# Another written-out order for the first 18 pairs of an attention and MLP kernel, and one weight difference in two halves

## The chip, the cores and the metric

The kernel runs on one core of one Trainium2 chip. The metric is the device time of one execution in microseconds (us). All durations below come from one execution that was recorded by the profiler, or are the times of unrecorded runs where the text says so.

## The reference

Cosine attention over 8 batches of 12 heads, 448 positions and a head dimension of 64, followed by a two-layer MLP with a hard-swish between the layers. Everything comes in and goes out in float32.

```python
q_n = q / (norm(q, axis=-1) + 1e-06)            # q, k, v: (8, 12, 448, 64)
k_n = k / (norm(k, axis=-1) + 1e-06)
attn = softmax(q_n @ k_n.T / tau)                # tau = 0.1
x = (attn @ v), heads side by side               # (3584, 768)
h = x @ w_in                                     # w_in: (768, 2048)
g = h * clip(h + 3, 0, 6) / 6
out = g @ w_out                                  # w_out: (2048, 768)
```

## The kernel before, in words

**Pairs and items.** Two heads of one batch form a pair; there are 48 pairs, six to a batch. Queries and keys are loaded two pairs at a time. Each such load is an item: of the first fourteen items the even one of a twosome is q and the odd one k, so items 2d and 2d+1 serve pairs 2d and 2d+1. An item goes through these operations, named as in the plan below:

- LQ loads it (L197, SyncE's queue, 448 KB), LV loads the values of two pairs (L209, four transfers).
- SQ squares it (L224 on ACT, L226 on DVE or POOL), RE sums the squares over the head dimension (L238, DVE), NO makes the reciprocal norms of two items with four short activations (L254 to L257, ACT), NM multiplies by them into bf16 (L269, DVE or POOL).
- TR transposes it on TensorE (L314). Later items are transposed by a DMA instead (XD).
- CQ and CK, with CS for the rest of the keys, copy the transposed tiles out of PSUM (L334, L336, L364, L374).
- VC casts the values of one pair (L286 on DVE, L288 on POOL).

A pair then runs through SC.i.g, the score matmuls of its four groups of keys (L414, L417), EX.i.g, the exponentials (L435, ACT), VA.i.g, the product with the values (L457), and FI, which divides by the row sums (L477, L478, DVE). BK and CX bring the result of a pair, transposed, into the MLP's input xT (L495, L497, L336); XB and XP do it by DMA.

**The MLP.** A unit U is one step of it: six matmuls into one PSUM bank for one of sixteen tiles of the hidden layer (L568), or, for the last six of the 36 units within the plan, sixteen matmuls of the second layer (L615). UA is its first evacuation on ACT (L577), UV the one on DVE (L583, or L628), which frees the bank. A unit of the first batch needs xT of pairs 0 to 5 complete and its part of w_in loaded; W issues one of eight weight transfers from POOL's queue (L911).

**Banks.** Up to pair 5 the scores use two double banks in turn. OPEN closes these and opens a ring of six single banks, which the scores (two banks a group), the transposes and the units take in turn. TensorE waits for the next bank in the ring until whoever read it last is done.

**Strassen's products.** From batch 1 on the second layer is computed by seven products of half-size blocks instead of eight. They need sums and differences of blocks of w_out, made once on DVE: WS (L690). The sums 1, 6 and 7 have tiles of their own; the differences y3 and y4, for the products M3 and M4, overwrite blocks of w_out, and so come after the last unit that still reads those blocks. GL copies the last columns of a batch's hidden layer to the next (L559).

**What sets the order.** For pairs 0 to 17 the order is written out by hand as a list of strings, `PLAN`. Tokens are executed in the order written, each recording its instructions on its engine; an engine then works its instructions off in that order, waiting where data or buffers are missing. A token's last letter names the engine where there is a choice: p is POOL, v DVE, a ACT. `DP.n` issues n matmuls of zeros into the PV bank (L923), 248 columns each, and `D.n` n of 512 columns into Y (L918): dummies, with no use of their result. From pair 18 (`FIRST`) on a loop sets the order; the table `side` lists the extra DVE operations of each round, and in round 18 that is y4.

Of the kernel before, what the change touches and what calls it, by code (L numbers as in the profile page):

```python
# [18 lines left out]
ORDER = "111111111111111111111111111111222222"  # L19

PLAN = [
    "LQ.1 DP.5 SQ.1.a.11.3 SQ.1.p.4.3 DP.1 SQ.1.a.0.4 LQ.0 SQ.0.p.8.6 DP.2 DP.4 LQ.3 LQ.2 SQ.1.v.7.4 RE.1.1",
    "SQ.0.a.0.6 RE.1.0 NO.0.1 LQ.5 LQ.4 SQ.0.v.6.2 DP.6 NM.1.p.0 D.10 RE.0.1 DP.3 NM.1.p.1 RE.0.0 DP.8",
    "NO.0.0 SQ.3.a.0.7 LV.0 DP.2 SQ.2.a.0.7 NM.0.p.0 RE.3 RE.2 NM.0.p.1 TR.1.Y DP.2 TR.0.Z CK.0.v DP.4 SQ.4.p.0.7 CQ.0.v",
    "SQ.5.a.0.7 LQ.6 NO.1 LV.1 LQ.7 SC.0.0.0 SC.0.1.1 DP.5 DP.3 CQ.1.v EX.0.0 RE.5 RE.4 NM.3.p SC.0.2.0 CK.1.v",
    "DP.3 EX.0.1 DP.3 EX.0.2 NM.2.v DP.3 SC.0.3.1 TR.3.Y LQ.8 NO.2 EX.0.3 DP.3 SC.1.0.0 TR.2.Z EX.1.0 VC.0.v",
    "SC.1.1.1 DP.2 EX.1.1 VA.0.0 CK.2.v VC.1.v VC.3.v NM.4.p NM.5.p VA.0.1 LQ.9 SC.1.2.0 SQ.6.a.0.7 LQ.11 DP.5",
    "DP.2 SC.1.3.1 EX.1.2 CQ.2.v LQ.10 LV.2 VA.0.2 VA.0.3 DP.3 SC.2.0.0 DP.2 EX.1.3 CK.3.v SC.2.1.1 EX.2.0 TR.4.Y",
    "SC.2.2.0 SQ.7.p.0.7 EX.2.1 RE.6 FI.0 RE.7 LV.3 VA.1.0 SQ.8.p.0.7 SC.2.3.1 CQ.3.v VC.2.v CQ.5.v VA.1.1 EX.2.2",
    "SC.3.0.0 EX.2.3 VA.1.2 NO.3 RE.8 SC.3.1.1 CQ.4.v EX.3.0 DP.2 DP.4 EX.3.1 VA.1.3 TR.5.Z SC.3.2.0 W SQ.9.p.0.7",  # L30
    "EX.3.2 FI.1 CK.4.v BK.0.Y VA.2.0 SC.3.3.1 RE.9 LV.4 EX.3.3 NO.4 VA.2.1 VA.2.2 VA.2.3 SC.4.0.0 EX.4.0 NM.6.p",
    "DP.2 SC.4.1.1 SQ.10.p.0.7 W SQ.11.p.0.7 EX.4.1 CX.0.v TR.6.Y CK.5.v FI.2 CQ.7.v VA.3.0 BK.2.Z RE.10 SC.4.2.0",
    "EX.4.2 NM.7.p CQ.6.v VA.3.1 SC.4.3.1 DP.2 EX.4.3 CX.2.v SC.5.0.0 RE.11 VA.3.2 EX.5.0 SC.5.1.1 VA.3.3 VC.4.p",
    "SC.5.2.0 FI.3 VC.5.p EX.5.1 BK.1.Y TR.7.Z SC.5.3.1 CX.1.v CK.6.v CK.7.v VA.4.0 EX.5.2 DP.2 CS.7.v EX.5.3",
    "BK.3.Y VA.4.1 LQ.12 CS.6.v OPEN DP.2 CX.3.v NO.5 SC.6.0 VA.4.2 VA.4.3 SC.6.1 SC.6.2 EX.6.0 NM.8.p FI.4 EX.6.1",
    "EX.6.2 SC.6.3 TR.8 BK.4 VA.5.0 CX.4.v VA.5.1 CQ.8.v SC.7.0 VA.5.2 EX.6.3 NM.9.p CQ.9.v VC.6.p VA.5.3 SC.7.1",
    "FI.5 EX.7.0 SC.7.2 TR.9 SC.7.3 NM.10.p CK.8.v VA.6.0 EX.7.1 EX.7.2 VC.8.p CS.8.v W BK.5 SQ.12.p.0.7 LQ.13",
    "VA.6.1 VA.6.2 SC.8.0 EX.7.3 CS.9.v VA.6.3 CK.9.v DP.1 EX.8.0 CX.5.v SC.8.1 SC.8.2 VC.7.p FI.6 LQ.15 EX.8.1 U",
    "UA SQ.13.a.0.7 LV.5 U TR.10 EX.8.2 UA U RE.13 U SC.8.3 UV UA CQ.10.v VA.7.0 W RE.12 UV CQ.11.a UV UA NO.6 U",
    "EX.8.3 VA.7.1 VA.7.2 UV VC.9.p VA.7.3 NM.11.p SC.9.0 FI.7 NM.12.p UA SC.9.1 UV EX.9.0 U VA.8.0 SC.9.2 EX.9.1",  # L40
    "VC.10.p UA SC.9.3 TR.11 UV NM.13.p CS.11.v XP.6 VA.8.1 LQ.14 EX.9.2 SQ.15.a.0.7 VA.8.2 U EX.9.3 CK.11.v",
    "CK.10.v VA.8.3 SC.10.0 TR.12 U CS.10.v FI.8 UA UV VA.9.0 SC.10.1 LQ.17 EX.10.0 SQ.14.p.0.7 CQ.12.v CQ.13.v",
    "SC.10.2 UA VA.9.1 LQ.19 VA.9.2 EX.10.1 LQ.16 VA.9.3 LV.6 W UV SC.10.3 EX.10.2 U SC.11.0 FI.9 EX.10.3 SC.11.1",
    "U UA EX.11.0 LV.7 EX.11.1 UV UA SC.11.2 RE.15 BK.8 LQ.18 CX.8.v U VA.10.0 U VA.10.1 UA EX.11.2 UV UV RE.14",
    "SC.11.3 UA BK.9 VA.10.2 VA.10.3 FI.10 EX.11.3 TR.13 NO.7 CK.13.v CS.13.v CX.9.a U UV CK.12.a VC.11.p W",
    "VA.11.0 U SC.12.0 CS.12.v VA.11.1 VA.11.2 UA BK.10 VA.11.3 UV UA NM.15.p UV EX.12.0 CX.10.v SC.12.1 EX.12.1",
    "SC.12.2 FI.11 U EX.12.2 BK.11 SC.12.3 UA NM.14.p SQ.16.p.0.6 U UA CX.11.v UV U SC.13.0 SQ.17.p.0.7 XD.14 UV",
    "RE.17 EX.12.3 VC.12.p EX.13.0 SQ.16.a.6.1 U UA RE.16 VC.15.p U VA.12.0 UV XD.15 UA U UA UA UV SC.13.1",
    "SQ.19.p.0.7 VC.13.p SC.13.2 UV EX.13.1 LQ.21 U VA.12.1 VA.12.2 UA UV RE.19 VA.12.3 EX.13.2 UV NO.8 W U",
    "SC.13.3 NM.16.p CK.15.v CK.14.v U UA UA SQ.18.a.0.7 EX.13.3 U SC.14.0 FI.12 UA VA.13.0 VC.14.p CS.14.v UV",  # L50
    "VA.13.1 UV EX.14.0 UV U SC.14.1 SC.14.2 VA.13.2 VA.13.3 UA EX.14.1 UV U W SC.14.3 FI.13 U VA.14.0 NM.17.p UA",
    "EX.14.2 UA VA.14.1 EX.14.3 XD.17 U UV VA.14.2 RE.18 SC.15.0 SC.15.1 UA UV EX.15.0 U XD.16 EX.15.1 UA UV",
    "VA.14.3 SC.15.2 U UA SC.15.3 EX.15.2 FI.14 NO.9 LV.8 VA.15.0 LV.9 UV CK.16.v UV EX.15.3 U SQ.21.p.0.7 VA.15.1",
    "RE.21 CS.16.v LQ.20 SC.16.0 LQ.22 SC.16.1 UA VC.16.p SC.16.2 VC.17.p VA.15.2 EX.16.0 VA.15.3 XP.12 NM.18.v",
    "CK.17.v XD.18 U EX.16.1 SQ.20.a.0.7 NM.19.p FI.15 WS.6 U UV XD.19 SC.16.3 RE.20 GL.0 WS.1 WS.7.0 EX.16.2 U VA.16.0 UA VA.16.1 LV.11",
    "EX.16.3 SC.17.0 UV VC.19.p SC.17.1 SC.17.2 SQ.22.v.0.7 VA.16.2 LQ.23 EX.17.0 VA.16.3 EX.17.1 LV.10 U SC.17.3",
    "XP.14 NO.10 FI.16 NM.20.p CK.18.v U CK.19.v WS.7.1 WS.y3 XB.16 EX.17.2 UV UA VA.17.0 VC.18.p EX.17.3 CS.18.v",
]


# [1038 lines left out]
```

## Time and profile before

| | us |
|---|---|
| median of 3 runs | 406.69 |
| lowest and highest | 406.35, 407.81 |
| the profiled execution | 406.46 |
| its span, first to last instruction | 404.6 |
| start of the first transpose on TensorE (TR.1) | 9.32 |
| start of the first exponential (EX.0.0) | 13.13 |
| start of the first unit (U) | 43.11 |

The granted clock of TensorE is 1.000 over the span. The span is 1.86 us shorter than the execution that it belongs to.

How to read the rows that follow: a row of the timeline gives the start in us from the span's first instruction, the length of the merged group, engine, line, operation, tiles as output<-inputs, shape, how many (x18), and in brackets how long the engine had been idle before and what ended the wait. A row of the busy time by stage gives the stretch, its length, and the busy us (and number of instructions) of PE, PEld (weight loads), DVE, ACT and POOL, then TensorE's granted clock, the share of the DMA engines and GB/s. A matmul's recorded length includes the time until its result has drained, so consecutive matmuls overlap; what one costs TensorE is the distance between two starts.

### The profile page before, as it was taken

What the parts mean: (1) busy time and instruction counts of PE and PEld (TensorE: products, weight loads), DVE (VectorE), ACT (ScalarE), POOL (GpSimd) and SP (SyncE); (2) the same over time, 40 slices, a digit from 0 to 9 for tenths busy, and PEclk for the clock granted to TensorE, in tenths of its full rate; (3) what the DMA queues carried; (4) which work ended last, traced back from release to release, by engine and by line L of the source; (5) the groups of instructions that cost most, each with busy time, mean ns of one, the idle gap of its engine ahead of it and who ended that gap; (6) DMA issues with size and microseconds to landing.
All of it is one profiled execution on the core that took longest, in us unless ns stands there. A gap on an engine that the chain in (4) does not pass through costs nothing.

```text
span 404.6 us, 9618 instructions
## 1 busy us (share of the span) xinstructions
PE 395.0 (98%) x3696; PEld 233.7 (58%) x3696; DVE 286.3 (71%) x502; ACT 278.6 (69%) x609; POOL 233.7 (58%) x228
## 2 busy tenths in 40 slices
PE   7899999999999999999999999999999999999996
PEld 5566656555655555655555556556565556555564
DVE  5898768766988777776857887587656666655663
ACT  5999998798467687687768768768758755225230
POOL 7799654662374996579485874876674600510070
PEclk9999999999999999999999999999999999999999
DMA  8999989979798749887789649986863522130134
GB/s 286 278 252 268 215 241 235 149 125 229 172 209 206 168 112 210 191 210 151 178 198 215 141 133 177 183 198 138 185 168 76 112 45 61 41 83 19 26 74 99
DMA packets 91566, 65.32 MB, mean 161 GB/s; under 512 B 56064, under 2 KB 89984, under 8 KB 91520
## 3 DMA queue, kind: packets, MB, share of 16 engines
q1 hardware_dynamic: 87408, 58.02, 62.5%
q0 software_dynamic: 3712, 6.29, 8.9%
q8 instruction: 29, 0.48, 0.5%
q10 hardware_dynamic: 400, 0.39, 0.3%
q14 instruction: 17, 0.14, 0.1%
HBM read 47.19 MB, written 11.01 MB: 144 GB/s over the span
## 4 chain that ended last, share of the span: by engine, by line
PE 91%; DVE 4%; DMA 3%; issue 1%; ACT 1%; SPq 0%; POOL 0%; DVEq 0%; POOLq 0%; ACTq 0%
PE M L568 23%; PE M L741 16%; PE PV L457 12%; PE Y L568 6%; PE M L417 6%; PE Z L568 5%; PE Y L741 4%; PE Z L741 3%; PE M L615 3%; PE M L821 2%; PE PV L923 1%; DVE n L238 1%; PE Z L417 1%; PE Z L821 1%; PE Y L417 1%; PE SC L417 1%
## 5 line engine op out<-in xcount | busy, mean ns | idle before, releaser
L435 ACT ACTIVATE at<-M 128x448 bf16<-128x448 f32 x200 | 99.6, 566 | 16.4 <-PE M L417 14.4
L568 PE MATMUL M<-xT,w_in_sb 128*128 128x448 bf16 x522 | 110.8, 352 | 0.0
L568 PEld LDWEIGHTS <-w_in_sb 128*128 128x128 bf16 x768 | 71.9, 98 | 62.6 <-issue 2.8
L269 POOL TENSOR_TENSOR nrm<-big,r 128x896 bf16<-128x896 f32 (+1 forms) x48 | 80.4, 1680 | 25.5 <-ACT r L257 18.1
L577 ACT ACTIVATE u<-M,bias 128x448 bf16<-128x448 f32 x87 | 56.9, 654 | 25.4 <-PE M L568 24.8
L583 DVE SCALAR_TENSOR_TENSOR gT<-u,M 128x448 bf16<-128x448 bf16 x76 | 46.9, 619 | 37.8 <-ACT u L577 37.1
L226 POOL TENSOR_TENSOR big<-big 128x896 f32<-128x896 f32 (+3 forms) x39 | 63.6, 1634 | 13.1 <-DMA big<-in_k_dram 5.5
L457 PEld LDWEIGHTS <-at 128*128 128x128 bf16 (+1 forms) x1536 | 54.8, 97 | 22.8 <-issue 13.5
L457 PE MATMUL PV<-vx,at 128*128 128x65 bf16 (+1 forms) x1536 | 64.3, 194 | 0.2 <-DVE on L478 0.2
L238 DVE TENSOR_REDUCE n<-big 128x14 f32<-128x896 f32 (+1 forms) x50 | 51.7, 1041 | 5.0 <-ACT big L224 4.6
L374 POOL COPY km<-tT 64x128 bf16<-64x128 bf16 x34 | 12.2, 358 | 58.2 <-DMA tT<-nrm 42.2
L770 POOL TENSOR_TENSOR big<-big 128x384 f32<-128x384 f32 x11 | 11.9, 1086 | 54.5 <-ACT big L789 54.4
L741 PEld LDWEIGHTS <-gT 128*128 128x128 bf16 x288 | 27.7, 98 | 21.0 <-DVE gT L583 1.2
L741 PE MATMUL M<-w_out_sb,gT 128*128 128x384 bf16 x208 | 37.9, 326 | 0.0
L435 ACT ACTIVATE at<-Z 128x448 bf16<-128x448 f32 x49 | 27.6, 563 | 9.9 <-PE M L417 9.6
L478 DVE TENSOR_TENSOR on<-PV,rc 128x512 bf16<-128x512 f32 x48 | 33.2, 692 | 1.7
L288 POOL CAST vx<-big 128x512 bf16<-128x512 f32 x44 | 32.8, 750 | 1.6 <-DMA big<-in_v_dram 1.5
L417 PE MATMUL M<-tT,kz 64*128 64x448 bf16 (+1 forms) x175 | 31.8, 351 | 0.2 <-DVE o L766 0.2
L741 PEld LDWEIGHTS <-gs 128*128 128x128 bf16 x224 | 21.5, 98 | 14.9 <-DVE gs L719 0.4
L568 PE MATMUL Y<-xT,w_in_sb 128*128 128x448 bf16 x132 | 28.6, 353 | 0.0
L435 ACT ACTIVATE at<-Y 128x448 bf16<-128x448 f32 x45 | 25.6, 568 | 3.1 <-PE Z L417 2.9
L741 PE MATMUL M<-w_sum,gs 128*128 128x384 bf16 x144 | 26.3, 326 | 0.0
(133 smaller groups left out, 560.7 us busy)
## 6 DMA issues: line engine op xcount, KB each, us to landing
big<-in_v_dram SPq DMA_DIRECT2D x96, 128.0 KB, 4.8
big<-in_k_dram SPq DMA_DIRECT2D x24, 448.0 KB, 5.0
big<-in_q_dram SPq DMA_DIRECT2D x24, 448.0 KB, 4.3
...
tT<-nrm SPq DMA_TRANSPOSE x34, 3.4
xT<-on SPq DMA_TRANSPOSE x25, 3.9
```

The lines of the kernel that those rows point to most:

```text
L226: engines[e].tensor_tensor(out=o, in0=i, in1=i, op=ALU.mult)
L238: nc.vector.tensor_reduce(out=n2s[d % 2][:, j % 2, c], in_=sq[:, :, :, :].rearrange("p g c d -> p (g c) d")[:, c, :], axis=AX.X, op=ALU.add,)
L269: engines[e].tensor_tensor(out=nrm[:, :, g, :].rearrange("p c g d -> p g c d"), in0=raw_of[j][:, g, :, :], in1=rs[d % 2][3][:, j % 2, :] . ...
L288: (engines[e].copy if e == "a" else engines[e].tensor_copy)(out=o, in_=f)
L417: nc.tensor.matmul(o, ks, qt[rows], start=True, stop=True)
L435: nc.scalar.activation(out=o, in_=x, func=AF.Exp, scale=inv_tau)
L457: nc.tensor.matmul(pv_out(j, h), at[rows, n, q_cols(i // HP, j)], vt[rows, 3 + h if name == "M" else 5 * h + int(name[1]), :], start=(name ...
L478: nc.vector.tensor_tensor(out=on[:, :, :, :].rearrange("p j h d -> p h j d"), in0=pv4[:, :, :, 0:D], in1=rc[:, :, :].to_broadcast([128, 2, ...
L568: nc.tensor.matmul(ps[:, 0:S], w_in_sb[:, cc, fc * 128 : (fc + 1) * 128], x[:, cc, 0:S], start=(cc == 0), stop=(cc == CC - 1),)
L577: nc.scalar.activation(out=u[:, :], in_=ps[:, 0:S], func=AF.Relu, bias=half_bias, scale=1.0 / 6.0)
L583: nc.vector.scalar_tensor_tensor(out=g[:, fc, c0 : c0 + S], in0=u[:, :], scalar=1.0, in1=ps[:, 0:S], op0=ALU.min, op1=ALU.mult,)
L741: nc.tensor.matmul(m, lhs[:, c, :], rhs[:, c, c0 : c0 + width], start=(base is None and c == 0), stop=(c == KC - 1), skip_group_check=True,)
```

## The change

The 36 lines of `PLAN` are replaced by 35 others: nearly the same operations in another order, some on another engine. The other edit is one entry of the table `side`. Line numbers behind the plan are one lower in the changed kernel.

```diff
 PLAN = [
-    "LQ.1 DP.5 SQ.1.a.11.3 SQ.1.p.4.3 DP.1 SQ.1.a.0.4 LQ.0 SQ.0.p.8.6 DP.2 DP.4 LQ.3 LQ.2 SQ.1.v.7.4 RE.1.1",
-    "SQ.0.a.0.6 RE.1.0 NO.0.1 LQ.5 LQ.4 SQ.0.v.6.2 DP.6 NM.1.p.0 D.10 RE.0.1 DP.3 NM.1.p.1 RE.0.0 DP.8",
-    "NO.0.0 SQ.3.a.0.7 LV.0 DP.2 SQ.2.a.0.7 NM.0.p.0 RE.3 RE.2 NM.0.p.1 TR.1.Y DP.2 TR.0.Z CK.0.v DP.4 SQ.4.p.0.7 CQ.0.v",
...
-    "EX.6.2 SC.6.3 TR.8 BK.4 VA.5.0 CX.4.v VA.5.1 CQ.8.v SC.7.0 VA.5.2 EX.6.3 NM.9.p CQ.9.v VC.6.p VA.5.3 SC.7.1",
-    "FI.5 EX.7.0 SC.7.2 TR.9 SC.7.3 NM.10.p CK.8.v VA.6.0 EX.7.1 EX.7.2 VC.8.p CS.8.v W BK.5 SQ.12.p.0.7 LQ.13",
-    "VA.6.1 VA.6.2 SC.8.0 EX.7.3 CS.9.v VA.6.3 CK.9.v DP.1 EX.8.0 CX.5.v SC.8.1 SC.8.2 VC.7.p FI.6 LQ.15 EX.8.1 U",
...
-    "XP.14 NO.10 FI.16 NM.20.p CK.18.v U CK.19.v WS.7.1 WS.y3 XB.16 EX.17.2 UV UA VA.17.0 VC.18.p EX.17.3 CS.18.v",
+    "DP.15 DP.4 DP.4 LQ.1 SQ.1.a.11.3 SQ.1.p.4.3 SQ.1.a.0.4 DP.6 LQ.0 SQ.1.v.7.4 RE.1.0 SQ.0.a.0.6 SQ.0.v.6.2 RE.1.1",
+    "SQ.0.p.8.6 LQ.2 RE.0.1 DP.24 RE.0.0 LQ.3 LV.0 NO.0.1 SQ.2.p.0.7 DP.3 NM.1.v.0 NO.0.0 NM.1.v.1 DP.6 LQ.4 TR.1.Y",
+    "NM.0.v.1 SQ.3.a.0.7 NM.0.v.0 DP.3 TR.0.Z CK.0.v VC.1.p VC.0.p CQ.0.v DP.4 SC.0.0.0 SC.0.1.1 LQ.5 RE.2 DP.5 RE.3",
+    "EX.0.0 EX.0.1 DP.2 SC.0.2.0 SQ.4.p.0.7 CK.1.v EX.0.2 NO.1 DP.4 SC.0.3.1 EX.0.3 VA.0.0 CQ.1.v VA.0.1 RE.4",
+    "SC.1.0.0 DP.1 LQ.7 EX.1.0 NM.3.v DP.6 SC.1.1.1 SQ.5.p.0.7 RE.5 VA.0.2 NM.2.p VA.0.3 EX.1.1 FI.0 SC.1.2.0 TR.3.Y",
+    "EX.1.2 TR.2.Z SQ.7.p.0.7 CQ.2.v SC.1.3.1 VA.1.0 NO.2 CK.2.v EX.1.3 VA.1.1 CK.3.v SC.2.0.0 BK.0.Y CQ.3.v LQ.6",
+    "EX.2.0 LV.1 SC.2.1.1 LV.2 NM.4.p W LQ.9 VA.1.2 LQ.8 VA.1.3 SC.2.2.0 EX.2.1 EX.2.2 SQ.6.v.0.7 VC.2.p TR.4.Z",
+    "SC.2.3.1 CX.0.v LQ.10 FI.1 EX.2.3 DP.2 SC.3.0.0 VA.2.0 SC.3.1.1 VA.2.1 EX.3.0 CQ.4.v VA.2.2 EX.3.1 SC.3.2.0 LV.3",
+    "CQ.5.v VA.2.3 NM.5.p BK.1.Y RE.7 TR.5.Z RE.6 VC.3.p EX.3.2 LQ.12 FI.2 NO.3 SC.3.3.1 DP.1 VA.3.0 CK.4.v W",
+    "SQ.9.p.0.7 SC.4.0.0 EX.3.3 CK.5.v VA.3.1 SQ.8.p.0.7 CX.1.v VC.4.p NM.6.v SC.4.1.1 EX.4.0 LV.4 VA.3.2 SC.4.2.0",
+    "VA.3.3 NM.7.p EX.4.1 VC.5.p BK.2.Z TR.6.Y SC.4.3.1 EX.4.2 RE.9 FI.3 CQ.6.v CQ.7.a SC.5.0.0 RE.8 VA.4.0 LQ.11",
...
+    "FI.4 OPEN BK.3.Y CK.6.v VA.5.0 CS.7.v SC.6.0 NO.4 VA.5.1 CX.3.v VC.6.p VA.5.2 EX.6.0 VA.5.3 CS.6.v CK.7.v BK.4",
+    "SC.6.1 FI.5 SC.6.2 CX.4.v SC.6.3 EX.6.1 NM.8.p VA.6.0 BK.5 EX.6.2 EX.6.3 TR.8 SC.7.0 VA.6.1 VC.7.v LQ.13 EX.7.0",
+    "VA.6.2 NM.9.p CX.5.v VC.8.p CQ.8.v W SC.7.1 EX.7.1 CQ.9.v SC.7.2 TR.9 VA.6.3 EX.7.2 RE.10 SC.7.3 LV.5 U CK.8.v",
+    "CK.9.v UA U CS.8.v FI.6 SQ.11.p.0.7 EX.7.3 SQ.12.p.0.7 SC.8.0 CS.9.v RE.11 SC.8.1 VC.9.p VA.7.0 UA VA.7.1 VA.7.2",
+    "EX.8.0 VA.7.3 LQ.14 NO.5 LQ.16 UV UV U EX.8.1 LQ.15 SC.8.2 EX.8.2 SC.8.3 FI.7 U RE.12 UA U EX.8.3 UA UA",
+    "SQ.13.v.0.7 UV SC.9.0 W SC.9.1 VA.8.0 VA.8.1 UV VA.8.2 VA.8.3 EX.9.0 W XP.6 UV EX.9.1 SC.9.2 RE.13 NM.11.p",
+    "NM.10.p TR.11 SC.9.3 EX.9.2 TR.10 FI.8 CS.10.v U NO.6 CQ.10.v EX.9.3 CK.10.v LQ.17 U CS.11.v VA.9.0 VA.9.1",
+    "CK.11.v SC.10.0 SQ.15.p.0.7 W UA UA NM.12.p CQ.11.v VA.9.2 VA.9.3 UV SC.10.1 UV SC.10.2 EX.10.0 U EX.10.1 RE.15",
+    "EX.10.2 LV.6 VC.11.p NM.13.p UA FI.9 SC.10.3 SC.11.0 EX.10.3 EX.11.0 SQ.14.v.0.7 U VC.10.p LQ.19 UV RE.14",
...
+    "XP.14 UA SC.17.1 NM.19.v SC.17.2 SQ.22.p.0.7 EX.17.0 EX.17.1 VA.16.2 VA.16.3 VC.18.v FI.16 U EX.17.2 XD.19",
+    "SC.17.3 CK.18.v XB.16 CK.19.v EX.17.3 GL.0 U UV WS.7.1 WS.y3 UA U LQ.23 NM.20.v UV CS.18.v VA.17.0 WS.y4.0",
 ]
...
-        18: [(weight_sums, "y4", 0, KC)], 19: sums(0, "62"), 20: sums(0, "1"),
+        18: [(weight_sums, "y4", KC // 2, KC // 2)], 19: sums(0, "62"), 20: sums(0, "1"),
```

Counted over the whole plan: both have 36 units, 33 evacuations of each kind, 72 groups of scores and of exponentials, and 14 transposes on TensorE. Of the 29 squares, ACT has 5 where it had 12, POOL 18 where it had 14, DVE 6 where it had 3. Of the 23 multiplies (halves counted singly), DVE has 8 where it had 2, POOL 15 where it had 21. Of the 20 casts of values, DVE has 5 where it had 4. The dummies are 90 of 248 columns, where they were 86 of 248 and 10 of 512 columns. The first U stands behind SC.7.3, where it stood behind SC.8.2. The first half of y4 is made at the end of the plan, the second in round 18 of the loop.

## The prediction

> **What bounds the kernel now.** The page first: who is busy.
>
> ```profile
> PE 395.0 (98%) x3696; PEld 233.7 (58%) x3696; DVE 286.3 (71%) x502; ACT 278.6 (69%) x609; POOL 233.7 (58%) x228
> ```
>
> TensorE is the bound of the whole, but only pairs 0 to 17 and one table entry are touched, so the second view is the busy time by stage. Its columns are PE, PEld, DVE, ACT and POOL, then the granted clock.
>
> ```profile
> 10.00:43.00 33.00, 30.92 (x433) 20.35 (x432) 29.15 (x65) 31.34 (x63) 30.55 (x25) 1.00 1.07 264
> 43.00:66.00 23.00, 23.00 (x254) 13.64 (x253) 16.36 (x32) 21.56 (x48) 10.78 (x11) 1.00 1.02 226
> 66.00:96.00 30.00, 30.00 (x290) 16.54 (x287) 21.57 (x41) 24.89 (x56) 17.34 (x16) 1.00 0.96 167
> 96.00:116.00 20.00, 20.00 (x186) 12.40 (x184) 18.64 (x22) 12.14 (x30) 9.84 (x8) 1.00 0.81 195
> 116.00:130.00 14.00, 13.12 (x124) 7.25 (x119) 11.50 (x17) 10.78 (x25) 7.44 (x9) 1.00 0.99 200
> ```
>
> From 43 us on PE is full. Before 43 ACT, POOL and DVE are each at 88% or more, and PE's 94% is flattered: a matmul's record contains its drain. So the third view is the timeline of PE, read by the distance between starts.
>
> ```profile
> 2.47 3.48 PE L923 MATMUL PV<-xT 128*128 128x248 bf16 x18 [2.47 <-DVE vx L976]
> ...
> 9.32 0.56 PE L314 MATMUL Y<-ident,nrm 128*128 128x128 bf16 x7
> ...
> 43.11 2.44 PE L568 MATMUL M<-xT,w_in_sb 128*128 128x448 bf16 x12
> ```
>
> The first transpose (TR.1) starts at 9.32 and the first MLP unit (U) at 43.11. Work in between, at start-to-start distances (0.056 a transpose, 0.095 a score matmul, 0.029 a PV matmul), is 18.0 us; the dummies are 86 x 0.106 + 10 x 0.216 = 11.3 us; the rest up to 43.11 is waiting. **All that another order can win lies there, plus what PE loses later.** The largest later loss is in the timeline at 120:
>
> ```profile
> 117.93 1.68 POOL L226 TENSOR_TENSOR big<-big 128x896 f32<-128x896 f32 x1 [1.25 <-DMA big<-in_q_dram]
> ...
> 118.27 2.96 DVE L690 TENSOR_TENSOR w_out_sb<-w_out_sb 128x3072 bf16<-128x3072 bf16 x1
> ...
> 121.15 0.61 DVE L583 SCALAR_TENSOR_TENSOR gT<-u,M 128x448 bf16<-128x448 bf16 x1
> ...
> 121.81 0.34 PE L741 MATMUL Z<-w_out_sb,gT 128*128 128x384 bf16 x1 [0.84 <-DVE gT L583]
> ```
>
> Product M3 has seven of its eight chunks done by 120.81 and waits 1.00 us for the last gT tile, whose DVE operation stands behind the M4 difference (L690).
>
> **A row that prices the swaps between POOL and DVE.** The same sum on DVE is short or long:
>
> ```profile
> 101.23 3.06 DVE L690 TENSOR_TENSOR w_sum<-w_out_sb 128x3072 bf16<-128x3072 bf16 x1
> ...
> 106.00 2.62 DVE L690 TENSOR_TENSOR w_sum<-w_out_sb 128x3072 bf16<-128x3072 bf16 x2
> ```
>
> ```profile
> 100.99 1.68 POOL L269 TENSOR_TENSOR nrm<-big,r 128x896 bf16<-128x896 f32 x1
> 102.62 2.14 POOL L288 CAST vx<-big 128x512 bf16<-128x512 f32 x1
> ```
>
> With POOL idle, a whole and a half sum take 2.62 together, so some 1.7 and 0.9. With POOL busy, one takes 3.06: it begins at 101.23, POOL's multiply ends at 102.6, 1.7 later (104.3) it is done, and POOL's cast, 0.60 elsewhere, takes 2.14, to 104.8. Each waits out the other's whole instruction. The same fits at 118.27: POOL's square ends at 119.6, and 1.65 later the difference is done. DVE's reductions show none of it (1.07 to 1.09 throughout).
>
> **The change, part by part.** Distances used: exps of 128x896 0.86 and of 128x448 0.43 (eight in 6.04 from 29.26 to 35.30); a NO 1.07 (15.54 to 16.61); POOL's square or multiply 1.65, its cast 0.60; on DVE a reduction 1.00, a FI 0.87, a copy 0.30, a square or multiply 1.05 (rows of 1.08, and 1.26 where POOL was busy); a U 1.135.
>
> 1. *Dummies.* 90 small ones for 86 and 10 large: 9.5 us for 11.3. That is no gain by itself, as they fill waits. But 62 stand ahead of TR.1 where 31 and the ten large stood: 6.57 for 5.45 us, so TR.1 starts no earlier than 10.44.
>
> 2. *Start to the first exp.* The four half multiplies of items 1 and 0 go from POOL (3.63 us in all) to DVE, at 0.54 each behind four half reductions that end near 8.4: 8.5 to 10.7, unless POOL's casts of pairs 1 and 0 come between (0.60 twice, to 11.9). Transposes, two copies and four dummies follow: first scores at 12.15 to 12.8 (before 12.73), first exp at 12.45 to 13.1 (before 13.13). I take 12.7.
>
> 3. *To pair 6.* Two squares leave ACT ahead of the first exp (item 2's for POOL, 5's behind it) and one later (SQ.6, to DVE); NO.1 moves behind the first exp, and ACT takes copy CQ.7. From the first exp to the last of pair 5 ACT then owes 6 x 3.0 + 3 x 1.07 + 0.43 = 21.7, against 22.1 before. DVE, though, gets NM.3, SQ.6 and NM.6, and gives up four casts and NM.2. Followed queue by queue: SQ.4 and SQ.5 run on POOL to 16.55, NM.3 on DVE to 17.6, NM.2 to 19.25; pair 2's exps start at 20.85 (before 21.31). SQ.6 is ready at 21.0, just after POOL began NM.4 (20.95 to 22.6), so it ends at 23.6. Behind it on DVE stand CX.0, FI.1, two copies, RE.7 and RE.6, which end at 27.4; NO.3 waits for RE.6, so ACT idles 1.0 us. Pair 4's exps start at 28.95 (before 29.26). NM.6 waits likewise for SQ.8 (30.5) and ends at 31.5; TR.6, CQ.7 and EX.4.3 wait for it, another 0.45. Pair 6's exps start at 36.95 (before 36.38).
>
> 4. *The first U.* It now stands behind SC.7.3, where it stood behind SC.8.2. Its bank is the one that the first half of EX.7.1 frees, ten exps after 36.95: 41.25, so it starts at 41.35. Ahead of it are six score matmuls fewer (0.57). The gain here is 43.11 - 0.57 - 41.35 = **1.2 us**. xT (last copy at 40.3) and the first weights (issued near 23 and 27, landing 7.6 to 13.8 later) are there.
>
> 5. *Pairs 7 to 12.* U are spread thinner: 11 ahead of SC.12.0, for 14. DVE owes, by these distances, 31 us in pairs 7 to 12 where PE owes 29.5; before, it was 24 for 31 in pairs 8 to 12. PE waits where an evacuation on DVE is late: 0.4 for CS.9, 0.4 for U1's, 0.7 for U3's (SQ.13 behind POOL's NM.11), 1.0 for the cast of pair 10 (SQ.14 and POOL exclude each other); smaller waits make up 0.3. SC.10.0 comes at 55.75 (before 55.27, with two PV groups less done), SC.12.0 at 66.1. In before it is the row
>
> ```profile
> 68.96 0.36 PE L417 MATMUL M<-tT,kz 64*128 64x448 bf16 x2
> ```
>
> with 3 x 1.135 + 0.21 - 0.70 = 2.9 us more work done: an equal 66.05. **The 1.2 is given back.** Without any waiting between POOL and DVE, SQ.6 ends 1.6 earlier, the first U comes at 39.9 and PE stays full: 2.65 gained. Between 0 and 2.65 I take 0.4, near the first, whose waits have rows; not 0, since SQ.6 misses its slot by 0.05.
>
> [...]
>
> 6. *Pairs 12 to 17.* PE owes 47 us, DVE 40 to 45. The six weight sums meet a POOL with little to do in pairs 15 to 17, so they should take nearer 1.7 than 3. NM.19 and NM.20 go to DVE (2.1). Nothing on either side: bound -0.5 to +0.5, value 0.
>
> 7. *The M4 difference in halves.* The first half runs after the last U, in the 1.28 us in which DVE waited for pair 17's values; the second behind FI.17. If it waits for POOL's square as before (to 119.6), it ends near 120.5, and gT at 121.05: PE waits 0.25 for 1.00. **Gain 0.75**; 1.0 if POOL isn't in the way, 0 if DVE comes 1 us late into its first half (its last stretch, from GL.0 on, is some 8 us for PE's 7).
>
> Sum: 406.46 (profiled: span 404.6 and 1.86 around it) - 0.4 - 0.75 = 405.3. The median of the runs is 0.23 above the profiled one, so **405.5**.
>
> **Rivals.**
> - *A, forecast*: the early U is paid back by DVE. 404.5 to 406.6. Chance 0.48.
> - *B, POOL and DVE miss each other*: the first U at 39.9, PE full behind it: 406.46 - 2.65 - 0.75 = 403.1. For it: ACT owes less and its starts are ahead up to pair 4. Against: the 3.06 and 2.14 rows. Chance 0.32.
> - *C, DVE becomes the bound in pairs 7 to 12*: I charge SQ.6, NM.6, SQ.13 and SQ.14 with 1.6, 1.25, 0.55 and 0.45 of waiting; with a whole POOL instruction (1.65) each, 2.75 more. All of it reaches PE, since evacuations stand behind: 406.46 + 2.75 - 0.75 = 408.5. It is slower than before once these waits grow by 0.75. Chance 0.16.
> - *D, TensorE's clock falls*: only 3 dummies are left after 17.7, where before 29 ran. The first 14 dummies of before ran at 0.201 to 0.207 for 0.106: the clock can be at half. If it were so from 20 to 41, PE's work there (some 14 us) would double and fill the stage: about 3 lost, 408.7. Against: no gap in the walk above exceeds 1.7 us, and before's gaps of 1.2 us cost no rate. Chance 0.04. [...]
>
> A measurement of this kernel tells about 0.5%, 2.03 us, from no change. Faster by more: B but for its upper edge, and A's lower edge, 0.34. Slower by more: D and most of C, 0.18. Between: 0.48. The range runs from B to C, 402.9 to 408.4, leaving B's and C's outer halves out.
>
> **What would show it.** First exp at 12.45 to 13.1; first U at 41.35 (B: 39.9); SQ.6 and NM.6 on DVE over 2 us long (B: 1.1); SC.12.0 at 66.1 (B: 63.4); L690's last half under 2.3 us and M3's last chunk waiting under 0.3. I am wrong if a DMA sets the early starts (V of pairs 0 and 1 is now issued ahead of items 4 and 5, and DMA share is 1.07 there), or if the fourth w_in part, issued near 46, lands after the ninth U wants it at 58.

## The result, and the profile after

| | before | after |
|---|---|---|
| median, measured side by side | 407.66 | 416.57 |
| lowest and highest | 406.35, 408.83 | 416.31, 417.86 |
| the profiled execution, its span | 406.46, 404.6 | 416.39, 414.6 |
| first transpose (TR.1), first exponential | 9.32, 13.13 | 11.64, 13.79 |
| first unit (U) | 43.11 | 43.80 |
| lost by TensorE, 20 to 40 us | 5.8 | 8.4 |
| 40 to 60 | 2.1 | 4.6 |
| 60 to 90 | 2.2 | 10.1 |
| 110 to 130 | 2.0 | 1.1 |

The changed kernel is slower: the ratio is 1.0231 (95% interval 1.0200 to 1.0261). The forecast was 405.5. The last four rows are worked out from the trace: the distance from one matmul to the next, less what the same shapes cost back to back (0.189 for a unit's matmul, 0.095 and 0.0775 for scores, 0.029 for values, 0.106 for a dummy, whose record is 0.269 long), summed over the stretch. They are called the loss below. Later stretches of 20 us agree within 0.6. The ratios, here and in the experiments, leave out executions more than 1.5% above the fastest of their kernel; the medians keep them.

The page's first line and the busy time by stage of the changed kernel answer to those of before.

```profile
PE 396.4 (96%) x3690; PEld 235.5 (57%) x3690; DVE 296.8 (72%) x512; ACT 274.2 (66%) x603; POOL 233.1 (56%) x225
```

```profile
10.00:43.00 33.00, 29.03 (x411) 19.62 (x409) 30.48 (x57) 25.82 (x52) 28.44 (x23) 1.00 1.00 264
43.00:66.00 23.00, 20.87 (x244) 12.09 (x243) 22.03 (x40) 19.77 (x49) 16.23 (x15) 1.00 1.13 214
66.00:96.00 30.00, 24.28 (x222) 13.28 (x221) 18.30 (x34) 20.20 (x45) 15.87 (x15) 0.94 1.01 211
```

PE was full from 43 on; now it misses 2.1 us up to 66 and 5.7 up to 96, and there the granted clock is 0.94. DVE is at 96% from 43 to 66 (71% before). From 66 to 96 no engine is full. The DMA engines' share there is 1.01, little more than before (0.96), so the share alone does not tell why; the chain below does. PE's timeline, as in the prediction:

```profile
2.48 9.32 PE L922 MATMUL PV<-xT 128*128 128x248 bf16 x62 [2.48 <-DVE vx L975]
11.64 0.55 PE L313 MATMUL Y<-ident,nrm 128*128 128x128 bf16 x7
...
43.80 2.43 PE L567 MATMUL M<-xT,w_in_sb 128*128 128x448 bf16 x12
```

The first U stands behind six score matmuls fewer (0.57), so the start lost 43.80 - 42.54 = 1.26 us where it was to gain 1.2. The chain of waits, followed back from 100 us, tells of the rest (start, length, what was under way; the long pieces alone):

```profile
49.04 3.36 POOL nrm L268 x2
52.41 14.97 DMA big<-in_q_dram
67.40 7.39 DMA big<-in_v_dram
...
75.13 1.71 POOL nrm L268
76.86 7.88 DMA tT<-nrm
84.76 0.35 DVE kz L363
85.11 0.54 DVE gT L582
85.69 1.81 PE M L567 x6
```

Thirty of the 36 us from 49 to 85 are three transfers: the load of item 17 (issued 52.41, 14.97 us), a load of values (7.39) and item 14's transposing transfer (7.88). CK.14 on DVE needs the last, and the gate product of a unit (UV) stands behind it in DVE's queue.

```profile
84.76 0.35 DVE L363 COPY kz<-tT 128x384 bf16<-128x384 bf16 x1 [4.64 <-DMA tT<-nrm]
```

```profile
85.69 1.81 PE L567 MATMUL M<-xT,w_in_sb 128*128 128x448 bf16 x6 [3.32 <-DVE gT L582]
```

PE is idle for 3.3 us meanwhile, and the stretch behind that runs at half clock (0.5 from 86.33 to 89.74). The busy time in steps of 2 us, same columns:

```profile
82.00:84.00 2.00, 0.38 (x2) 0.10 (x1) 0.00 (x0) 0.63 (x1) 0.00 (x0) 1.00 1.34 110
84.00:86.00 2.00, 0.31 (x2) 0.19 (x2) 1.21 (x4) 0.00 (x0) 0.00 (x0) 1.00 1.09 323
86.00:88.00 2.00, 2.00 (x15) 1.09 (x13) 2.00 (x3) 0.46 (x1) 1.83 (x2) 0.58 1.10 232
88.00:90.00 2.00, 2.00 (x7) 0.85 (x6) 1.19 (x2) 1.04 (x3) 1.86 (x3) 0.56 1.37 314
```

What ran beside the long transfers is seen in the DMA issues from 50 to 90 us (count, size, median us from issue to landing). Before:

```profile
w_out_sb<-in_moe_w_out_dram POOLq DMA_DIRECT2D x4, 768.0 KB, 9.2
...
big<-in_q_dram SPq DMA_DIRECT2D x3, 448.0 KB, 5.9
big<-in_v_dram SPq DMA_DIRECT2D x8, 128.0 KB, 7.0
tT<-nrm SPq DMA_TRANSPOSE x4, 5.8
xT<-on SPq DMA_TRANSPOSE x1, 4.1
```

After:

```profile
w_out_sb<-in_moe_w_out_dram POOLq DMA_DIRECT2D x3, 768.0 KB, 9.8
big<-in_v_dram SPq DMA_DIRECT2D x16, 128.0 KB, 7.6
big<-in_q_dram SPq DMA_DIRECT2D x3, 448.0 KB, 11.7
...
tT<-nrm SPq DMA_TRANSPOSE x2, 8.2
xT<-on SPq DMA_TRANSPOSE x1, 14.9
```

The four w_out transfers were issued at 60, 61, 78 and 86 us; now they are at 48, 58, 71 and 74, ahead of loads that are needed sooner. POOL's queue moved 2.91 MB in these 40 us and now 4.16, SyncE's 4.52 and now 4.68.

**The first theory** was this: w_out's early transfers hold up loads and transposing transfers, the queues of POOL and DVE, worked off in order, carry that to PE (4.64 us of waiting on DVE, 3.32 on PE), and the clock falls behind the gap. **Rivals**: VectorE (DVE in the rows) and POOL exclude each other (SQ.13 takes 3.48 us on DVE); the late start throws the rest out of step; the order behind pair 8 stalls whatever the transfers do.

### The profile page after: what moved, and what is told of

Its sections match the earlier page's. It is cut to its first block, busy times and chain, and to the rows that moved or that the text cites. A ratio compares the mean times of both kernels' runs of the same rounds, so it can differ in the third digit from the quotient of the medians.

```text
span 414.6 us, 9606 instructions
## 1 busy us (share of the span) xinstructions
PE 396.4 (96%) x3690; PEld 235.5 (57%) x3690; DVE 296.8 (72%) x512; ACT 274.2 (66%) x603; POOL 233.1 (56%) x225
## 4 chain that ended last, share of the span: by engine, by line
PE 80%; DMA 9%; POOL 4%; DVE 4%; issue 1%; SPq 1%; ACT 0%; POOLq 0%; DVEq 0%
PE M L567 21%; PE M L740 17%; PE PV L456 10%; PE Y L567 5%; PE Z L567 5%; PE M L416 5%; PE Y L740 4%; PE Z L740 4%; DMA big<-in_q_dram 4%; DMA big<-in_v_dram 3%; PE M L614 3%; DMA tT<-nrm 2%; PE M L820 2%; POOL nrm L268 2%; PE Z L820 1%; POOL big L225 1%
## 5 line engine op out<-in xcount | busy, mean ns | idle before, releaser
L434 ACT ACTIVATE at<-M 128x448 bf16<-128x448 f32 x197 | 97.8, 565 | 18.8 <-PE M L416 16.6
L225 POOL TENSOR_TENSOR big<-big 128x896 f32<-128x896 f32 (+4 forms) x43 | 70.7, 1650 | 36.2 <-DMA big<-in_k_dram 15.8
L268 POOL TENSOR_TENSOR nrm<-big,r 128x896 bf16<-128x896 f32 x42 | 72.0, 1719 | 10.7 <-ACT r L256 8.2
L373 POOL COPY km<-tT 64x128 bf16<-64x128 bf16 x34 | 15.1, 443 | 53.0 <-DMA tT<-nrm 29.8
L769 POOL TENSOR_TENSOR big<-big 128x384 f32<-128x384 f32 x11 | 11.8, 1071 | 54.7 <-ACT big L788 54.7
L287 POOL CAST vx<-big 128x512 bf16<-128x512 f32 x43 | 30.1, 700 | 8.7 <-DMA big<-in_v_dram 8.7
L434 ACT ACTIVATE at<-Y 128x448 bf16<-128x448 f32 x48 | 27.1, 565 | 3.4 <-PE Z L416 3.2
L567 PE MATMUL Z<-xT,w_in_sb 128*128 128x448 bf16 x126 | 27.3, 352 | 0.1
```

Source lines behind the costliest of these rows:

```text
L225: engines[e].tensor_tensor(out=o, in0=i, in1=i, op=ALU.mult)
L268: engines[e].tensor_tensor(out=nrm[:, :, g, :].rearrange("p c g d -> p g c d"), in0=raw_of[j][:, g, :, :], in1=rs[d % 2][3][:, j % 2, :] . ...
L287: (engines[e].copy if e == "a" else engines[e].tensor_copy)(out=o, in_=f)
L434: nc.scalar.activation(out=o, in_=x, func=AF.Exp, scale=inv_tau)
L567: nc.tensor.matmul(ps[:, 0:S], w_in_sb[:, cc, fc * 128 : (fc + 1) * 128], x[:, cc, 0:S], start=(cc == 0), stop=(cc == CC - 1),)
```

## The experiments

Each ratio is to the kernel before on the same chip, with its 95% interval. Short diffs show tokens of the plan.

**The M4 halves alone**, in the kernel before.

```diff
-        18: [(weight_sums, "y4", 0, KC)], ...
+        18: [(weight_sums, "y4", KC // 2, KC // 2)], ...      # and "WS.y4.0" at the end of PLAN
```

> The kernel before with the second part of the change alone: the plan's order is untouched, the first half of y4 stands at its end, the second in round 18. In the trace of the changed kernel M3's eight chunks run without a gap where before showed 1.00 us. Theory: the halves are worth 0.75 to 1.0 us by themselves, so 0.2% under the kernel before, and M3's gap is gone. Rival: the gap went in the changed kernel only because POOL is idle around its M4 difference (whole sums take 1.75 there for 3.0); then here, where POOL is busy as in before, DVE is late into its first half and the time is that of before within 0.3 us.

Measured 405.64 for 406.06, 0.9978 (0.9959 to 0.9997): 0.4 us gained. PE's timeline shows product M3 whole, all eight chunks from 119.33, and a new wait behind it:

```profile
119.33 1.74 PE L741 MATMUL Z<-w_out_sb,gT 128*128 128x384 bf16 x8
...
127.02 0.35 PE L568 MATMUL M<-xT,w_in_sb 128*128 128x448 bf16 x1 [0.58 <-DMA xT<-on]
```

The 1.00 us wait is gone, and 0.58 comes back as a wait for a transfer into xT. The second half does meet POOL: 2.23 us where the changed kernel's takes 0.95. This is the only version here that beats the kernel before, by 0.2%, with an interval that just leaves out 1.

**The w_out transfers later.** w_late moves them, w_late_ws also a weight sum that reads them.

```diff
- ... EX.9.0 W XP.6 ... SQ.15.p.0.7 W UA ... FI.10 W U ... EX.12.1 W U ...
+ ... CX.9.v XD.14 W ... VA.13.0 W SC.13.3 ... XD.15 W ... VA.13.2 W EX.14.0 ...
- ... UV WS.7.0 CS.14.v ...        # w_late_ws only
+ ... WS.1 WS.7.0 ...              # w_late_ws only
```

> The changed kernel with its four w_out transfers issued behind XD.14 (some 80 to 92 us) in place of 48, 58, 71 and 74 us; nothing else moved. Theory of the transfers: three weight transfers within 5 us (43.0, 47.6, 48.2) and two more at 71 and 74 slow the q and v loads (LQ.17 took 15 us to land, a V load over 7, the transposing DMA XD.14 7.9), and that is the loss of 69 to 90 us: 1.3 + 1.35 + 3.5 in three stalls and some 1.4 at half clock behind the longest. They go, the granted clock stays 1.000, and the time falls by 6 to 8 us, to 1.003 to 1.008 of before. Theory of POOL and DVE excluding each other as the main cause: the loads only look slow because their buffers come free late; the time stays within 2 us of the changed kernel's (1.018 to 1.026 of before).

> The changed kernel with its four w_out transfers issued where w_late had them (behind XD.14, VA.13.0, XD.15 and VA.13.2), and the weight sum WS.7.0, which w_late left waiting 9.3 us on VectorE for them, moved behind WS.1. Theory of the transfers (w_out's early transfers hold up the loads of q and v and the transposing transfer of item 14, and the 3.3 us stall of TensorE at 82 and the half clock behind it follow from that): the stalls between 69 and 90 go, which together cost some 7 us, and 1.2 to 2.3 us of the start and of 49 remain: 408 to 411 us, a ratio of 1.003 to 1.012, granted clock 1.00. Rival, the later order itself (squares and multiplies that stand on VectorE and POOL in an order that waits): the stalls come back elsewhere, the ratio is 1.018 or more.

Measured 419.63, 1.0338 (1.0294 to 1.0381), and 416.95, 1.0258 (1.0226 to 1.0290). Neither theory's time was met by w_late; w_late_ws, by its time, is the rival's. In w_late_ws the stalls from 69 to 90 did go: the loss from 60 to 90 is 4.4 for 10.1. But in both a sum on DVE waited for w_out instead, in w_late WS.7.0:

```profile
90.18 0.96 DVE L690 TENSOR_TENSOR w_sum<-w_out_sb 128x1536 bf16<-128x1536 bf16 x1 [9.32 <-DMA w_out_sb<-in_moe_w_out_dram]
```

In w_late_ws it was WS.6, 7.79 us. The changed plan makes these sums in pairs 13 to 15, so it needs w_out early. The times therefore don't tell the theories apart; the stretch 60 to 90 of w_late_ws speaks for the first.

**w_out as in the kernel before, sums and all.**

```diff
+ ... LV.6 W VC.11.p ... W VA.11.0 ... NO.8 W ... W SC.14.3 ...
+ ... FI.15 WS.6 ... EX.16.3 WS.1 WS.7.0 ...
```

> The changed kernel with its four w_out transfers where the kernel before has them (behind LV.6, ahead of VA.11.0, behind NO.8, ahead of SC.14.3) and the weight sums that read them, WS.6, WS.1 and WS.7.0, in pair 16 as there. w_late and w_late_ws put the transfers still later and left sums early, and each ended in a wait for w_out. Theory that w_out ahead of the loads of q and v is the cause: the stalls from 60 to 90 go and nothing waits for w_out, 408 to 411 us, a ratio of 1.004 to 1.012, granted clock 1.00. Rival, that the changed order of the loads, squares and multiplies stalls by itself: 1.018 or more.

Measured 412.61, 1.0117 (1.0075 to 1.0160). By clock, the ten executions fall apart: four at 1.000 took 408.4 to 410.3 (a fifth 412.7), five at 0.992 to 0.995 took 412.5 to 415.1. All five of the changed kernel had 0.990 to 0.995. Judged by the clock, then, the stall comes in half the executions without early w_out, and not in all. In the profiled one (408.5) it did not: the loss from 60 to 90 is 3.9.

```profile
43.00:66.00 23.00, 22.34 (x256) 12.80 (x253) 21.80 (x42) 21.48 (x53) 18.24 (x16) 1.00 1.14 224
66.00:96.00 30.00, 29.07 (x282) 16.44 (x280) 22.12 (x41) 24.08 (x53) 18.17 (x18) 1.00 1.10 219
```

Two things limit what this shows. Its transfers from 50 to 90 us were not all quicker: the loads of q took 8.2 (11.7 in the changed kernel), those of v 7.7 (7.6), of k 9.7 (7.3). And the square SQ.13 on DVE, which took 3.48 in the changed kernel, took 1.71 here, so the edit also shortened a wait between DVE and POOL:

```profile
50.20 1.71 DVE L226 TENSOR_TENSOR big<-big 128x896 f32<-128x896 f32 x1
```

**w_out early in the kernel before.**

```diff
+ ... EX.9.0 W U ... SC.10.0 W TR.12 ... FI.10 W EX.11.3 ... EX.12.1 W ...      # and the four later W gone
```

> The kernel before with nothing changed but the issue of its four w_out transfers, put where the changed kernel has them (behind EX.9.0, SC.10.0, FI.10 and EX.12.1; about 48, 57, 71 and 74 us instead of 60, 61, 78 and 86). Theory of the transfers: loads of q of 15 us and transposing transfers of 7 us appear here too, with stalls of TensorE between 60 and 90: 2 to 6 us more, a ratio of 1.005 to 1.015. Rival, the transfers hurt only because the changed order lets what waits for them stand at the head of VectorE's and POOL's queues: within 1 us of before, 0.997 to 1.003.

Measured 407.31, 1.0030 (1.0000 to 1.0060). Two of ten executions had a clock under 0.997 and took 411 and 413; the others 406.0 to 409.2. With early transfers alone the stall is rare, and by the time the rival is nearer. Where it does come it looks as the theory has it: in the profiled execution (413.2) a load of k behind two w_out transfers took 22.55 us, and the loss from 60 to 90 was some 9 us.

```profile
55.39 22.55 DMA big<-in_k_dram
```

**No w_out traffic at all**, in both kernels.

```diff
     def next_weights():
         o, w = weights.pop(0)
-        nc.gpsimd.dma_start(out=o, in_=w)
+        if len(weights) < 4:
+            nc.gpsimd.memset(o, 0.01)
+        else:
+            nc.gpsimd.dma_start(out=o, in_=w)
```

> The changed kernel with the four transfers of w_out left out: POOL fills each part with a constant at the place where it issued the transfer, so the output is that of another w_out. 3.1 MB fewer pass the DMA engines between 48 and 91 us, and nothing else moves. Theory that w_out ahead of the loads of q and v makes most of the loss: no load of q above 9 us and no transposing transfer above 6 us from 50 to 90, the stalls there go, 405 to 409 us, a ratio of 0.998 to 1.008, granted clock 1.00. Rival, that the changed order of the steps loses by itself: 412 us or more, 1.015 or more.

> The kernel before with the same four transfers left out in the same way (the output is that of another w_out): what w_out's traffic costs there, to set beside no_wout_after. Theory: in the kernel before w_out comes when the loads that are next are already issued, so it costs next to nothing, 405 to 406.5 us, a ratio of 0.998 to 1.001. Rival, that the 3.1 MB cost both orders alike: 400 to 403 us, 0.985 to 0.993.

Measured 413.55, 1.0198 (1.0177 to 1.0218), and 407.45, 1.0043 (1.0022 to 1.0063): the time fits the rival. The trace says why. From 60 to 90 the loss fell to 4.1, and most transfers were quick (50 to 90 us), though not the one into xT:

```profile
big<-in_v_dram SPq DMA_DIRECT2D x16, 128.0 KB, 4.2
big<-in_q_dram SPq DMA_DIRECT2D x3, 448.0 KB, 4.9
...
tT<-nrm SPq DMA_TRANSPOSE x2, 4.0
xT<-on SPq DMA_TRANSPOSE x1, 9.9
```

So without w_out's traffic 6.0 of the 7.9 us lost there are gone, and the kernel before doesn't feel that traffic (2.1 for 2.2). But a constant fill keeps POOL for 2.66 us where issuing the transfer took 0.80, and that made another stall worse, from 40 to 60 us (7.3 for 4.6, half clock from 55.1 to 58.5 included): SQ.13 on DVE, here first in the changed kernel and then in this one, each with POOL beside it.

```profile
49.87 3.48 DVE L225 TENSOR_TENSOR big<-big 128x896 f32<-128x896 f32 x1
...
67.40 1.09 DVE L225 TENSOR_TENSOR big<-big 128x896 f32<-128x896 f32 x1 [0.65 <-DMA big<-in_q_dram]
```

```profile
49.04 3.35 POOL L268 TENSOR_TENSOR nrm<-big,r 128x896 bf16<-128x896 f32 x2
```

```profile
49.60 5.27 DVE L225 TENSOR_TENSOR big<-big 128x896 f32<-128x896 f32 x1
```

```profile
47.95 2.68 POOL L911 MEMSET w_out_sb<- 128x3072 bf16 x1
50.57 3.34 POOL L268 TENSOR_TENSOR nrm<-big,r 128x896 bf16<-128x896 f32 x2
```

Alone the square takes 1.09. In both it ends 0.96 us after POOL's last instruction (52.39 and 53.35; 53.91 and 54.87). PE, in the changed kernel, waited for the gate product behind the square:

```profile
53.93 0.37 PE L416 MATMUL M<-tT,kz 64*128 64x448 bf16 x2 [2.13 <-DVE gT L582]
```

The experiment thus measured two things at once, and by its time alone it would have misled.

**SQ.13 and SQ.14 on ACT.**

```diff
- SQ.13.v.0.7 ... SQ.14.v.0.7
+ SQ.13.a.0.7 ... SQ.14.a.0.7
```

> The changed kernel with squares 13 and 14 on ACT in place of DVE; nothing else. Theory of exclusion: the stall of 2.3 us at 49.4 (a square on DVE waits for two of POOL's multiplies, and the evacuations that free the banks stand behind it) goes; ACT pays 2 x 0.86, of which little is on the path. 1.5 to 3 us less than the changed kernel: 1.016 to 1.020 of before. Theory of the transfers: what is won at 49 is waited out at 67, where LQ.17's landing decides; within 0.7 us of the changed kernel.

Measured 418.66, 1.0295 (1.0248 to 1.0342). The loss from 40 to 60 fell from 4.6 to 3.1, and from 60 to 90 it rose from 10.1 to 13.1: item 17's load took 17.3 us, and PE waited 1.55 us at 62.5 for a part of w_in. What is won at 49 is waited out behind 60, and more: the time is above both forecasts. With w_late's places as well it took 418.68, 1.0310 (1.0271 to 1.0349), and waited for w_out as w_late did.

**Start and rest exchanged.** start_after and start_before change plans at OPEN, pairs8_after and pairs8_before at SC.8.1, where the two plans differ in nine steps.

```diff
+ pairs8_before:  <before's plan up to SC.8.1>  VC.7.v LV.5 U UA U FI.6 VC.9.p VA.7.0 ...  <after's rest>
+ pairs8_after:   <after's plan up to SC.8.1>  EX.8.0 NO.5 NM.10.p UA UV EX.8.1 LQ.15 UV SC.8.2 ...  <before's rest>
```

> The changed kernel's order up to the opening of the second stage's pools (OPEN), then the kernel before's order for all that is left, with the difference for M4 whole: the changed start alone. The start reaches OPEN with less done ahead (NO.4, SQ.11, RE.10 and RE.11 come behind it). Theory that the start costs by itself what the first U shows (0.7 to 1.3 us, and no gain later): 407 to 409 us, a ratio of 1.002 to 1.008. Rival, that the start costs nothing in the end because the steps behind it wait for other things: 1.000. Rival, that work left undone at OPEN is waited for again: above 1.008.

> The kernel before's order up to OPEN, then the changed kernel's order for all that is left, with the difference for M4 in halves. Theory of the transfers (the cost is made between 48 and 90 us and hardly depends on the start): 412 to 415 us, a ratio of 1.015 to 1.022, with TensorE's stall before the U's at some 80 us. Rival, that the late start shifted the later steps into the stalls: 405 to 408 us, 0.997 to 1.005.

> The changed order of pairs 0 to 7 (up to SC.8.1, three of stage two's first products included) and then the kernel before's order for the rest, with the difference for M4 whole. At this cut the two orders differ in nine steps, where start_after's cut left work standing that a 6.4 us stall then waited for. Theory that the changed order's cost is made behind pair 8: only what the first U shows is left (0.7 us on the span, some 1.3 at the second), 406.5 to 408.5 us, a ratio of 1.002 to 1.006. Rival, that the late start is what throws the rest out of step: 1.015 or more.

> The kernel before's order of pairs 0 to 7 (up to SC.8.1) and then the changed order for the rest, with the difference for M4 in halves. Theory that the cost is made behind pair 8: 413 to 417 us, a ratio of 1.018 to 1.027, though the start is the faster one. Rival, that the late start throws the rest out of step: 405 to 407 us, 0.997 to 1.003.

Measured: start_after 418.52, 1.0288 (1.0253 to 1.0323); start_before 416.85, 1.0271 (1.0232 to 1.0311); pairs8_after 413.37, 1.0163 (1.0119 to 1.0207); pairs8_before 416.35, 1.0226 (1.0178 to 1.0275). With the start of before, the changed rest costs as much as the whole change, so the start's 1.26 us don't show in the total. In pairs8_before a load of q issued behind the early w_out took 17.52 us. The other way round, the loss from 60 to 90 is that of before (2.4 and 2.6 for 2.2). Both of these lose elsewhere, start_after 6.2 us at once behind its cut and pairs8_after some 7 us from 40 to 60, where work that one plan had left for later was wanted by the other. By its time alone pairs8_after (1.0163) fits the rival; because of that loss these two times are no measure of the start.

**Before's first eight pairs and its places for w_out.**

> pairs8_before with w_out's transfers and sums moved as in w_before: the kernel before's first eight pairs, the changed order behind them, and the kernel before's places for w_out. Theory that w_out's transfers make the cost behind pair 8: 405 to 408 us, 0.997 to 1.005. Rival, that the rest of the changed order stalls by itself: 1.015 or more.

Measured 408.48, 1.0044 (1.0009 to 1.0078). Six of ten executions took 407.0 to 408.8 at 0.998 to 1.000, four 412.0 to 416.7 at 0.987 to 0.995: the median is 7.9 us below that of pairs8_before on the same chip, but the changed order still stalls now and then. The profiled execution (412.6) is one of the four, and its stall is of another kind. Its loads of q and v were not long (6.9 and 7.1). A square on DVE, SQ.17, took 6.70 us beside six instructions of POOL that followed one another from 63.3 to 70.4, and PE waited behind it, with half clock from 70.4 to 77.3:

```profile
63.21 6.70 DVE L226 TENSOR_TENSOR big<-big 128x896 f32<-128x896 f32 x1
```

```profile
71.47 0.55 PE L417 MATMUL Y<-tT,kz 64*128 64x448 bf16 x1 [4.73 <-DVE kz L336]
```

Here the rival of VectorE and POOL made the stall, with w_out at its old places. What made it in the three other executions is not recorded.

**Before's engines in the start.**

```diff
- SQ.2.p NM.1.v NM.0.v VC.1.p VC.0.p NM.3.v SQ.5.p NM.2.p SQ.6.v VC.2.p VC.3.p NM.6.v
+ SQ.2.a NM.1.p NM.0.p VC.1.v VC.0.v NM.3.p SQ.5.a NM.2.v SQ.6.a VC.2.v VC.3.v NM.6.p
```

> The changed kernel, its order kept, with the squares, multiplies and value casts ahead of OPEN on the engines that the kernel before gives them (items 0 and 1 multiplied on POOL, squares 2, 5 and 6 on ACT, NM.3 and NM.6 on POOL, NM.2 on VectorE, the casts of items 0 to 3 on VectorE). Theory that VectorE and POOL exclude each other in the start (0.93 us for a half multiply that takes 0.54 alone) and that this, not the order, made the first U late: NM halves of items 0 and 1 no longer stretched on VectorE, the first U at 41.5 to 42.8 us instead of 43.8; the total hardly moves, 415 to 417 us, since the loads behind 50 us take the gain back as in pairs8_before. Rival, that the order of the start itself is late: first U at 43.5 or later.

Measured 418.48, 1.0294 (1.0252 to 1.0336), the first U at 45.68. The number is the rival's, but the run does not test what it was built for. The casts of pairs 1 and 0, now on DVE ahead of the copy CQ.0, waited for their values, so the first exponential came at 14.72 (13.79 in the changed kernel):

```profile
12.69 1.28 DVE L285 TENSOR_REDUCE vx<-big 128x512 bf16<-128x512 f32 x2 [0.87 <-DMA big<-in_v_dram]
```

Then TensorE waited for NM.2 on DVE, and the clock was at half from 23.2 to 26.7. Whether the engines or the order make the start late stays open. A part lies behind OPEN: with before's order up to there (start_before) the first U, six score matmuls earlier in the plan, came at 43.34 and so was still late.

**CK.14 out of the way.**

```diff
- CX.11.v UV CK.14.v U UA ... WS.7.0 CS.14.v
+ CX.11.v UV U UA ... WS.7.0 CK.14.v CS.14.v
```

> The changed kernel with one step moved: CK.14, VectorE's copy out of the tile that item 14's transposing transfer fills, from behind CX.11 and a gate product to just ahead of CS.14, that is behind three more gate products and WS.7.0. Theory that the stall of 3.3 us at 82 is made by VectorE's queue, where CK.14 stands in front of gate products that nothing holds: the stall and the half clock behind it go, 5 us less than the changed kernel or a little under it, 411 to 413 us, a ratio of 1.012 to 1.017. Rival, that the loads are late for everything behind as well, so that the next step waits instead: 415 to 417 us, 1.020 to 1.026.

Measured 422.07, 1.0388 (1.0333 to 1.0442). The rival's mechanism holds, at more than its price: the transfer now took 10.07 us, PE waited 3.57 for it with its own scores,

```profile
93.78 0.37 PE L416 MATMUL M<-tT,kz 64*128 64x448 bf16 x2 [3.57 <-DMA tT<-nrm]
```

and another stall of 2.0 us at 75 brought a second stretch at half clock. DVE's queue passed the wait on; moving one step out of it did not take the wait away.

**The gap filled with dummies.**

```diff
- VC.15.p UA U SQ.18.p.0.7
+ VC.15.p UA DP.24 U SQ.18.p.0.7
```

> The changed kernel with 24 dummy products of 128x248 (0.106 us each in the start, 2.5 us in all) on TensorE ahead of the 17th U, the one that started at 85.69 us behind the stall. They run while TensorE would be idle and add nothing to the path as long as they end before 85.7. Theory that the half clock from 86 to 90 follows from the idle time itself: the granted clock stays 1.00 there, some 1.9 us less, 414 to 415 us, a ratio of 1.017 to 1.021. Rival, that the clock falls for another reason: the windows 86 to 90 stay at 0.50 to 0.67 and the time stays at 416 to 417.

Measured 418.69, 1.0312 (1.0266 to 1.0359). Inconclusive: in its profile the stall came 5 us earlier, ahead of the dummies (PE idle for 2.77 us from 77.28), with half clock from 79.8 on, and another from 55.9.

**All three together**: start_engines, w_before and ck14_late.

> start_engines, w_before and ck14_late together: the changed order with the kernel before's engines ahead of OPEN, its places for w_out's transfers and sums, and CK.14 behind three gate products. If the three causes are separate and are all there is: 404.5 to 407 us, a ratio of 0.995 to 1.002, with the granted clock at 1.00 in most executions. If the changed order of loads keeps a cost of its own: 408 to 412 us, 1.005 to 1.015, with part of the executions at a clock under 1.00.

Measured 410.39, 1.0101 (1.0050 to 1.0152). The time is that of the second case, but not all that remains is shown to be the loads: from 60 to 90 the loss is some 2.3 above the kernel before, and the start, with before's engines again at half clock from 23.1 to 26.6, has its first U at 44.60.

## Why the prediction was wrong, step by step

1. *Dummies.* "TR.1 starts no earlier than 10.44": 11.64, and 10.8 to 11.8 in the thirteen traces with the changed start. The bound held, but the first exp was then reckoned without it. I priced 62 dummies at the rate of before, but the full rate came at another time in each run: the dummies, 0.207 apart at first and 0.106 later, changed over at 5.4 us in the profile of before and at 7.8 in that of after (5.1 to 8.1 over all runs); 62 dummies fix TR.1 to that, 31 and ten large ones less so.
2. *First exp at 12.7*: 13.79. PE ran without a pause from the first dummy to TR.0 at 12.35, so the dummies of step 1 set it. The half multiplies were late as well: one of the four took 2.10 on DVE for my 0.54 (the others 0.61 to 0.63), beside POOL's square of item 2, and ended 0.48 behind that square; the last ended at 12.02. By my estimate they alone would have put the first exp some 0.3 earlier than it came. Mis-sized, with the mechanism of step 3 forgotten here.
3. *To pair 6, exps at 36.95*: 39.02. 1.1 came from step 2. SQ.6 took 2.37 to 24.45 (23.6), NM.6 2.09 to 32.07 (31.5), CQ.7 waited 1.47 for my 0.45. The waits for POOL were as forecast, each size short. The path of one was wrong: NO.3 did not idle ACT. ACT idled 1.31 us ahead of pair 3's exps, because two dummies in front of their scores need the PV bank, and FI.1, which frees it, stood on DVE behind SQ.6:

```profile
25.64 0.37 PE L922 MATMUL PV<-xT 128*128 128x248 bf16 x2 [1.22 <-DVE on L477]
```

4. *The first U, a gain of 1.2*: 1.26 lost, from 1 to 3.
5. *Pairs 7 to 12, SC.12.0 at 66.1*: 71.36. **The first failed step of the rest.** U3's wait behind SQ.13 was to be 0.7: PE waited 2.13 for that gate product, because SQ.13 ended only behind POOL's NM.11 and NM.10 together, where I let it in after one instruction. In w_late, w_late_ws, w_before and combined, with the same two multiplies beside it, it did get in after one (1.71 and 1.72), so this term turns on something that I had no row for. And item 17's load, which the chain shows ahead of everything from 52 on, is in no term of mine.
6. *Pairs 12 to 17, value 0, bound 0.5.* **The step that failed most**: some 5.6 us more (the span's 10.0, and 0.9 won behind it, less the 5.3 that SC.12.0 was late for equal work). I set the engines' owed time against PE's and did not follow the transfers, though my own fence had the DMA share at 1.02 and 0.96 there and the diff moved four transfers of 768 KB ahead of loads. With w_out's transfers issued early the loads beside them took longer (q 11.7 us for 5.9, and 4.9 without w_out), and the change had reordered them.
7. *The M4 halves, 0.75*: 0.42 alone, the gap of M3 gone as priced, 0.58 waited elsewhere. In the changed kernel the halves take 0.95 each, and the loss from 110 to 130 is 0.9 lower.

The pieces, on the span: 1.3 (start) + 2.3 (SQ.13) + 7.9 (60 to 90, of which some 1.7 is half clock) - 0.9 (M4) = 10.6 for the 10.0 measured.

Of the rivals, B fell with the rows for SQ.6 and SQ.13. C had the right sign and one right cause, at 0.16 and 8 us short. D came true outside the stretch that I gave it, from 86 on, and inside it only in start_engines and combined. My argument against D looked at the gaps of the start only. What I named as a possible mistake, a DMA that sets the early starts or w_in's fourth part landing late, looked at other transfers than those that cost most, w_out and q; the values did set the start in start_engines, and w_in was late in sq_act.

Shown: in the changed order w_out's early traffic makes 6 us of the loss between 60 and 90 (by the profiled executions of w_before and no_wout_after, 6.2 and 6.0), and the loss behind 60 belongs to the plan behind pair 8 (pairs8_before, pairs8_after). It takes both: by the clock, early w_out in the changed order stalled in five of five executions, in before's order in two of ten; the changed order with w_out at its old places in five and in four of ten. Not settled: what makes the stall in those nine, of which the one on record was a square on DVE beside POOL; what part the loads of v have, of which the changed kernel issues 16 pieces from 50 to 90 us where before issued 8; and which step of the start is late.
